# Attention and MoE kernel on one core: softmax probabilities scaled by other engines, two heads' scores in one pass, new order of work

## Chip, cores and metric

The kernel runs on one core of a Trainium2 chip. The metric is device time in microseconds (us) of one execution; lower is better. TensorE (PE) multiplies matrices, PEld is its loading of stationary operands, VectorE is DVE, ScalarE is ACT, GpSimd is POOL, and SP only issues DMAs.

## The reference, cut to what matters

Four batches, eight heads, 576 rows of 64 elements. Each head has causal softmax attention plus a memory read; the sum passes through a two-matrix block.

```python
scores = scale * np.matmul(q, k.transpose(0, 1, 3, 2))      # causal mask, softmax -> a
local = np.matmul(a, v)
q_p = phi(q)                                                # elu(q) + 1
mem_out = einsum(q_p, M_prev) / (einsum(q_p, z_prev) + 1e-6)
x = g * mem_out + (1 - g) * local                           # [2304, 512] after the heads are joined
h = x @ w_in                                                # 512 -> 2048
y = (np.maximum(h, 0) + alpha * np.minimum(h, 0)) @ w_out   # 2048 -> 512
```

## The kernel before

**Numbers.** Most matrix products are made of three or two f16 products of a high and a low half (`hi`, `lo`), because f16 streams through PE faster than f32. Early work, for which the weights and scales are not yet there, is done in plain f32: the first 64 rows of all batches (group Z), batch 0's scores, its first row blocks' transposes and values, and the first half (j < 4) of the MoE of the groups Z and (0, 1).

**Units.** A unit is (batch b, head h, two row blocks: [1, 2] or [3, 4]); there are 64. `unit_scores` (L825) makes both blocks' scores in PSUM, has DVE add the mask and find the minimum (`tensor_tensor_reduce` into the tile `E`), and ACT take the exponential with the row sum in `sm`. Batch 0's scores are f32 products over 64 rows of the array, one head after the other, in the PSUM tiles `s1` (512 words) and `s2` (1024 words). `unit_probs` (L866) finds 1/sum on DVE, and then POOL does two things for each block: it writes q's features times `nrm` into 64 columns of `E`, and it scales the exponentials by the reciprocal. ACT then casts all of `E` to f16 (`P[:, 0]`), DVE subtracts it for the low half (`P[:, 1]`), and SP issues a transposing DMA into `PT`. The units (0, h, [1, 2]) have no halves: PE transposes `E` into `s2`, ACT copies it out. `E` has two buffers of 1152 words. `pair_values` (L901) multiplies `PT` with the values for two heads in the PSUM tile `bank`, and the result goes through another transposing DMA to the group's `x`.

**MoE.** A group is 256 rows: (b, 1) and (b, 3) for each batch, and Z. `moe_in` (L1019) and `moe_out` (L1059) make one of eight steps j of a group. The weights arrive as raw pieces s = 0 to 15 (first half of the hidden width 0 to 7, second half 8 to 15). `conv_w(s)` (L575) makes f32 of piece s in `R[s+1]`, and `split_w(s)` (L607) makes its two f16 halves from `R[s+1]` in `fin(s)` = `R[s]`. So split s writes over the raw piece s-1, and the sixteen splits follow each other from 0 to 15. Steps j >= 4 of Z and (0, 1) need the second half's splits; all later groups need both halves.

**Order.** Operations are not issued as written. `Work.add` (L134) records each with its dependencies (a whole PSUM tile at once), `price` (L182) gives it a duration, `lay` (L241) lays all operations on the five queues, and `issue` (L308) orders them by rank plus the offsets of `STAGES` (L32), two passes forward and one back between them. The result is one fixed order for each engine's queue.

Of the kernel before, what the change touches and what calls it, by code (L numbers as in the profile page):

```python
# [33 lines left out]
        "A0": 11.3, "A:DVE": -217.6, "BK0": -98, "BK:ACT": 124.3, "BK:PE": -853.4, "C0": -90.5, "C1": 150,  # L34
        "C2": -98.2, "C3": -196.5, "C:DVE": 47.3, "C:PE": 107.6, "I": -14.7, "I:POOL": -120.8, "J": -112.4,
        "J:ACT": 4.9, "J:DVE": 0.6, "J:PE": -33.7, "K": -70.4, "K:POOL": 54.3, "L0K:DMA": 52.5, "L0Q": 2,
# [19 lines left out]
        "s33": 401.7, "s:ACT": 20.5, "s:DVE": 100, "s:PE": -311.2, "sZ": -745.5, "sZ:DVE": 63.5, "sZ:PE": 340.6,  # L56
# [4 lines left out]
        "y:DMA": -1030.3, "y:DVE": -62.5, "y:PE": 4032.8,  # L61
# [40 lines left out]
class Work:  # L102
# [30 lines left out]

    def add(self, kind, engine, name, a, kw):  # L134
# [10 lines left out]
        for x, write in [(x, False) for x in ins] + [(x, True) for x in outs]:  # L145
            if x.tensor.name in self.fixed:
                continue
            m, size = self.cells(x)
            if x.space == PSUM:

                m = (1 << 2 * size) - 1
            wrote, read = self.state.setdefault(x.tensor.name, ([], []))
            deps.update(o for o, c in wrote if c & m)
            if not write and x.space == PSUM:
                deps.update(o for o, c in read if self.ops[o][0] != kind)
            if not write:
                read.append((me, m))
                continue
            deps.update(o for o, c in read if c & m)
            for was in (wrote, read):  # L160
                was[:] = [(o, c & ~m) for o, c in was if c & ~m]
            wrote.append((me, m))
        deps.discard(me)
        if last:
# [4 lines left out]
            self.ops.append((kind, both, (a[0],), {}, deps, last[5] + 6, *last[6:]))  # L169
# [12 lines left out]
    def price(self, kind, name, outs, ins, kw):  # L182
# [34 lines left out]
        if kind == "POOL":  # L217
            if name == "tensor_scalar":
                return 150 + 1.55 * n
# [21 lines left out]
    def lay(self, before, after, rank, back=False):  # L241
# [11 lines left out]
        turn, used, warm = WINDOW, 0.0, False  # L253
# [4 lines left out]
        while todo:  # L258
# [49 lines left out]
    def issue(self, tc):  # L308
# [15 lines left out]
        for passes, bias in STAGES:  # L324
            rank = [x + 1e3 * (bias.get(op[7], 0) + bias.get(op[7].rstrip("0123456789_") + ":" + op[0], 0))
                    for x, op in zip(rank, ops)]
# [13 lines left out]
def kernel(  # L340
# [49 lines left out]
    o_sc = bank[:, 256:512]  # L390
    ident = cp.tile([128, 128], F32, name="ident")
# [31 lines left out]
    def fin(pos):  # L423
        return R[pos].bitcast(F16)
# [132 lines left out]
    wkp.made["E"] = [0, [E[:, 1152 * i:1152 * i + 1152] for i in range(2)]]  # L557
    E = E[:, 0:2048]
# [264 lines left out]
    flip = [0]  # L823

    def unit_scores(b, h, bl):  # L825
        work.phase = f"s{b}{bl[0]}"
        p = pre[b]
        a = h % 2
        width = [64 + 128 * i for i in bl]
        mx = smp.tile([128, 2], F32, tag="mx", bufs=3, name=f"mx{b}_{h}_{bl[0]}")  # L830
        sm = smp.tile([128, 2], F32, tag="sm", bufs=3, name=f"sm{b}_{h}_{bl[0]}")
        f32 = b == 0 and bl[0] == 1
        E = wkp.tile([128, 1152], F32, tag="E", name=f"E{b}_{h}_{bl[0]}")
        flip[0] ^= 1
        if sum(width) > 512:
            s1 = psp.tile([128, 512], F32, tag="s1", name=f"sa{b}_{h}")
            s2 = psp.tile([128, 1024], F32, tag="s2", name=f"sb{b}_{h}")
            where = [s1[:, 0:width[0]], s2[:, 0:width[1]]]
        else:
            u = 0 if f32 else flip[0]  # L840
            ps = psp.tile([128, (512, 1024)[u]], F32, tag=("s1", "s2")[u])
            where = [ps[:, 0:width[0]], ps[:, width[0]:sum(width)]]
        if b:
            qT, qS, k1, _ = stacks[b, h // 2]
            terms = [(qT[:, a], k1[:, a]), (qS[:, a], k1[:, a])]
        else:
            terms = [(x[64 * a:64 * a + 64, h // 2] for x in (p["qT"], p["kT"]))]
        terms = [tuple(x) for x in terms]
        for i, w, s in zip(bl, width, where):
            for c0 in range(0, w, 512):  # L850
                c1 = min(c0 + 512, w)
                for j, (x, y) in enumerate(terms):
                    T.matmul(s[:, c0:c1], lhsT=x[:, (i - 1) * 128:i * 128],
                             rhs=y[:, 64 + c0:64 + c1], start=(j == 0), stop=(j == len(terms) - 1))
        es, o = [], 0
        for j, (w, s) in enumerate(zip(width, where)):
            o += 64
            es.append(E[:, o:o + w])
            V.tensor_tensor_reduce(out=es[j], in0=s, in1=mask[:, 576 - w:576], op0=ALU.add, op1=ALU.min,
                                   scale=p["nse"] if b else -0.125, scalar=3.0e38, accum_out=mx[:, j:j + 1])  # L860
            o += w
        for j, e in enumerate(es):
            A.activation(e, e, AF.Exp, bias=mx[:, j:j + 1], scale=-1.0, accum_out=sm[:, j:j + 1])
        ust[b, h, bl[0]] = (sm, es, E)

    def unit_probs(b, h, bl):  # L866
        work.phase = f"P{b}{bl[0]}"
        p = pre[b]
        sm, es, E = ust.pop((b, h, bl[0]))
        nb = len(bl)  # L870
        V.scalar_tensor_tensor(out=sm, in0=sm, scalar=1e-9, in1=p["C"][:, h, bl[0] - 1:bl[-1]],
                               op0=ALU.add, op1=ALU.mult)
        V.reciprocal(sm, sm)
        ns = sum(i + 1 for i in bl)
        s0 = 0
        for j, i in enumerate(bl):
            G.tensor_scalar(E[:, s0 * 128:s0 * 128 + 64], nat[b]["q"][i - 1][:, h], p["nrm"][:, i - 1, h:h + 1], None,
                            op0=ALU.mult)
            G.tensor_scalar(es[j], es[j], sm[:, j:j + 1], None, op0=ALU.mult)
            s0 += i + 1  # L880
        if b == 0 and bl[0] == 1:
            PT = wkp.tile([128, 9, 128], F32, tag="PT", bufs=TB)
            pt = psp.tile([128, 1024], F32, tag="s2")[:, 0:128 * ns]
            for c in range(ns):
                T.transpose(pt[:, c * 128:c * 128 + 128], E[:, c * 128:c * 128 + 128], ident)
            A.copy(PT[:, 0:ns].rearrange("p s c -> p (s c)"), pt)
# [4 lines left out]
        E = E[:, 0:ns * 128]  # L891
        A.copy(P[:, 0], E)
# [444 lines left out]
```

## Time and profile before

| what | value |
|---|---|
| median of 3 runs | 629.15 us (624.66 to 632.19) |
| the profiled execution | 629.02 us, of which the span of the instructions is 627.2 us |
| mean granted TensorE clock | 0.965 of full |
| PE busy in the span | 566.9 us |
| DVE, ACT, POOL busy | 449.7, 357.8, 260.0 us |

Busy time of PE is the union of its records, whose ends are modelled; matmuls overlap in the pipeline, so the distance from start to start tells what one really takes. "Idle before" is time in which the engine had nothing running, with the operation that ended it.

### The profile page before, as it was taken

What the parts mean: (1) busy time and instruction counts of PE and PEld (TensorE: products, weight loads), DVE (VectorE), ACT (ScalarE), POOL (GpSimd) and SP (SyncE); (2) the same over time, 40 slices, a digit from 0 to 9 for tenths busy, and PEclk for the clock granted to TensorE, in tenths of its full rate; (3) what the DMA queues carried; (4) which work ended last, traced back from release to release, by engine and by line L of the source; (5) the groups of instructions that cost most, each with busy time, mean ns of one, the idle gap of its engine ahead of it and who ended that gap; (6) DMA issues with size and microseconds to landing.
All of it is one profiled execution on the core that took longest, in us unless ns stands there. A gap on an engine that the chain in (4) does not pass through costs nothing. (4 is left out here: it accounts for less than half of the span.)

```text
span 627.2 us, 11994 instructions
## 1 busy us (share of the span) xinstructions
PE 566.9 (90%) x4421; PEld 365.8 (58%) x4421; DVE 449.7 (72%) x1141; ACT 357.8 (57%) x710; POOL 260.0 (41%) x270
## 2 busy tenths in 40 slices
PE   9858999799899889988998798979889899999997
PEld 4447644463377556556665576557457566666663
DVE  2797898869878989888887888776766775323242
ACT  4437747647678736757466765576655664332222
POOL 2000486564543025655656652565676665000000
PEclk9958999999879999999999999998999999999999
DMA  7899555764359784656996942578725653210000
GB/s 215 217 306 222 174 168 150 205 148 106 84 125 197 172 210 100 127 96 143 178 221 146 191 86 55 118 152 168 152 56 102 130 119 86 47 43 0 18 18 33
DMA packets 226026, 82.84 MB, mean 132 GB/s; under 512 B 216224, under 2 KB 216240, under 8 KB 225968
## 3 DMA queue, kind: packets, MB, share of 16 engines
q1 hardware_dynamic: 225968, 82.09, 57.6%
q8 instruction: 34, 0.56, 0.4%
q14 instruction: 24, 0.20, 0.1%
HBM read 35.66 MB, written 5.77 MB: 66 GB/s over the span
## 5 line engine op out<-in xcount | busy, mean ns | idle before, releaser
L336 PE MATMUL h<-x,R 128*128 128x256 f16 x1536 | 264.2, 276 | 18.6 <-DVE r L336 13.6
L336 PE MATMUL y<-R,gg 128*128 128x512 f16 (+1 forms) x832 | 258.3, 400 | 5.0 <-ACT gg L336 3.8
L336 POOL TENSOR_SCALAR E<-E,sm 128x192 f32<-128x192 f32 (+3 forms) x128 | 184.0, 1450 | 90.6 <-DVE sm L336 62.5
L336 PE MATMUL bank<-v,PT 128*128 128x64 f16 x1224 | 186.9, 195 | 10.2 <-DVE xn L336 9.1
L336 PEld LDWEIGHTS <-R 128*128 128x128 f16 x1536 | 149.4, 99 | 58.5 <-DVE r L336 20.7
L336 POOL TENSOR_SCALAR E<-q,nrm 128x64 f32<-128x64 f32 x128 | 72.1, 576 | 181.6 <-DVE nrm L336 66.7
L336 PEld LDWEIGHTS <-PT 128*128 128x128 f16 x1224 | 116.5, 99 | 17.4 <-issue 10.9
L336 PEld LDWEIGHTS <-gg 128*128 128x128 f16 x768 | 74.6, 98 | 85.5 <-issue 7.5
L336 DVE TENSOR_TENSOR P<-E,P 128x1152 f16<-128x1152 f32 (+1 forms) x56 | 63.1, 1127 | 55.4 <-ACT P L336 55.4
L336 ACT CAST P<-E 128x1152 f16<-128x1152 f32 (+1 forms) x56 | 54.2, 968 | 84.4 <-POOL E L336 81.0
L336 ACT ACTIVATE E<-E,mx 128x192 f32<-128x192 f32 (+3 forms) x128 | 77.7, 608 | 35.8 <-DVE mx L336 35.6
L336 DVE SCALAR_TENSOR_TENSOR gg<-r,gsc,gg 128x512 f16<-128x512 f32 x56 | 42.1, 752 | 40.7 <-ACT gg L336 40.2
L336 PE MATMUL s<-k,qT 128*128 128x192 f16 (+8 forms) x200 | 66.6, 376 | 4.3 <-DVE mx L336 4.3
L336 DVE SCALAR_TENSOR_TENSOR r<-r,oma,h 128x256 f32<-128x256 f32 x128 | 55.9, 475 | 19.7 <-ACT r L336 19.3
L336 ACT ACTIVATE gg<-r,gsc 128x512 f16<-128x512 f32 x56 | 40.1, 717 | 47.7 <-PE y L336 46.2
L336 DVE CUSTOM_DVE_ANT_0 E<-s,mask,pm 128x320 f32<-128x320 f32 (+2 forms) x96 | 56.6, 611 | 5.0 <-PE s L336 4.3
L336 ACT ACTIVATE r<-h 128x512 f32<-128x512 f32 x72 | 42.0, 589 | 27.3 <-DVE gg L336 13.1
L336 PE MATMUL h<-R 128*128 128x256 f32 x128 | 34.8, 414 | 4.5 <-ACT R L336 3.4
L336 PE MATMUL s<-k,qS 128*128 128x192 f16 (+4 forms) x120 | 33.9, 294 | 0.3 <-DMA qS<-qT 0.3
L336 PEld LDWEIGHTS h<-R 128*128 128x128 f32 x128 | 25.1, 210 | 10.1 <-ACT R L336 4.5
L336 ACT ACTIVATION_READ_ACCUMULATOR E<-E,mx 128x1 f32 x128 | 24.1, 188 | 0.0
L336 PE MATMUL h<-ones 128*128 128x512 f16 x66 | 21.3, 423 | 1.0 <-DVE ones L336 1.0
(173 smaller groups left out, 614.5 us busy)
## 6 DMA issues: line engine op xcount, KB each, us to landing
vn<-in_v_dram SPq DMA_DIRECT2D x16, 256.0 KB, 4.2
q<-in_q_dram SPq DMA_DIRECT2D x16, 256.0 KB, 5.4
out_dram<-t SPq DMA_DIRECT2D x16, 256.0 KB, 2.2
kn<-in_moe_w_in_dram SPq DMA_DIRECT2D x6, 512.0 KB, 5.8
kn<-in_moe_w_out_dram SPq DMA_DIRECT2D x6, 512.0 KB, 4.3
kn<-in_k_dram SPq DMA_DIRECT2D x12, 256.0 KB, 4.3
qS<-qT SPq DMA_DIRECT2D x24, 128.0 KB, 2.9
R<-in_moe_w_in_dram SPq DMA_DIRECT2D x4, 512.0 KB, 6.9
```

What stands on the lines that cost most here:

```text
L336: fn(*a, **kw)
```

## The change

1. `unit_probs`: POOL no longer scales the exponentials. It writes only the features, now with two scalar factors (`nrm` and the sum times the constant `sm`), and the reciprocal goes to a second tile `rs`. ACT scales while it writes the high half and DVE scales while it subtracts, each in two instructions, one a block, instead of one for both. For the units (0, h, [1, 2]) ACT scales the f32 exponentials in place.
2. `first_pair`: batch 0's scores of two heads are issued side by side, head a on array rows 64a to 64a+63, in different PSUM banks. For [3, 4] block 4 of one head stands beside block 3 of the other.
3. PSUM: `s1` and `s2` become one tile `SS` of three banks, and dependencies in PSUM are kept by bank. Blocks [1, 2] of later batches and the two steps of group Z take turns in the three banks. The f32 transposes go through one bank in two portions (four and one).
4. `E` of the units (0, h, [1, 2]) gets five tiles of 640 words: three in the old place and the two `P` buffers.
5. `fin(0)` moves to `R[16]` and `fin(8)` to `R[0]`; batch 0's f32 `x32` moves from `R[16]` to `R[0]`. `weights(1)` with its splits 8 to 15 now stands ahead of `splits(0)` and `splits(4)`, and the chain of overwrites runs from 8 to 15 and then 0 to 7.
6. The planner prices POOL's `tensor_scalar` at 290 + 2.55 n instead of 150 + 1.55 n ns, adds a price for changing between whole-array and partial-array matmuls, and has a second set of offsets, by phase and engine. All queues get another order.

```diff
 STAGES = [
     (2, {
-        "A0": 11.3, "A:DVE": -217.6, "BK0": -98, "BK:ACT": 124.3, "BK:PE": -853.4, "C0": -90.5, "C1": 150,
+        "A0": -271.6, "A:DVE": -630.1, "BK0": 128.2, "BK:ACT": 57.8, "C0": -243.2, "C1": 111.2, "C2": -388.2,
...
+    (1, {
+        "A0": -7.3, "A0:DVE": -0.1, "A:DVE": 26.5, "BK0": -47.7, "BK0:ACT": 3.9, "BK0:PE": -0.6, "BK:ACT": 7.7,
...
-            m, size = self.cells(x)
-            if x.space == PSUM:
-
-                m = (1 << 2 * size) - 1
+            m = self.banks(x) if x.space == PSUM else self.cells(x)[0]
...
-                return 150 + 1.55 * n
+                return 290 + 2.55 * n
...
+                    if packets != mode:
+                        hold += (95 if packets else 0) + (0, 0, 150, 200)[mode]
+                    mode = packets
...
     def fin(pos):
-        return R[pos].bitcast(F16)
+        return R[{0: 16, 8: 0}.get(pos, pos)].bitcast(F16)
...
+    wkp.made["E3"] = [0, [E[:, 768 * i:768 * i + 640] for i in range(3)] + [x[:, 0:640] for x in wkp.made["P"][1]]]
...
+    def first_pair(hp, bl):
+        work.phase = f"s0{bl[0]}"
+        p = pre[0]
+        tiles = [unit_tiles(0, 2 * hp + a, bl) for a in range(2)]
+        for j in range(2):
+            cols = []
+            for a in range(2):
+                i = bl[j if bl[0] == 1 else a ^ j ^ 1]
+                w = 64 + 128 * i
+                o = 512 * a + 192 * j if bl[0] == 1 else 1024 if i == 3 else 0
+                cols.append((a, i, SS[:, o:o + w]))
+            cols.sort(key=lambda x: -x[2].shape[1])
+            for c0 in (0, 512):
+                for n, (a, i, row) in enumerate(cols):
+                    c1 = min(c0 + 512, row.shape[1])
+                    if c1 <= c0:
+                        continue
+                    x, y = (p[t][64 * a:64 * a + 64, hp] for t in ("qT", "kT"))
+                    work.paired = n == 1
+                    T.matmul(row[:, c0:c1], lhsT=x[:, (i - 1) * 128:i * 128], rhs=y[:, 64 + c0:64 + c1],
+                             start=True, stop=True)
+            for a, i, row in cols:
+                es, mx, _ = tiles[a]
+                e = i - bl[0]
+                lowest(0, row, es[e], mx[:, e:e + 1])
...
-            G.tensor_scalar(E[:, s0 * 128:s0 * 128 + 64], nat[b]["q"][i - 1][:, h], p["nrm"][:, i - 1, h:h + 1], None,
-                            op0=ALU.mult)
-            G.tensor_scalar(es[j], es[j], sm[:, j:j + 1], None, op0=ALU.mult)
+            G.tensor_scalar(E[:, s0 * 128:s0 * 128 + 64], nat[b]["q"][i - 1][:, h], p["nrm"][:, i - 1, h:h + 1],
+                            None if f32 else sm[:, j:j + 1], op0=ALU.mult, op1=ALU.bypass if f32 else ALU.mult)
+            if f32:
+                A.activation(es[j], es[j], AF.Copy, scale=rs[:, j:j + 1])
+            segs.append(slice(s0 * 128, (s0 + i + 1) * 128))
...
-        A.copy(P[:, 0], E)
-        V.tensor_tensor(P[:, 1], E, P[:, 0], op=ALU.subtract)
+        for j, c in enumerate(segs):
+            A.activation(P[:, 0, c], E[:, c], AF.Copy, scale=rs[:, j:j + 1])
+            V.scalar_tensor_tensor(out=P[:, 1, c], in0=E[:, c], scalar=rs[:, j:j + 1], in1=P[:, 0, c],
+                                   op0=ALU.mult, op1=ALU.subtract)
...
-            groups[b, i].update(x32=R[13 if b else 16].rearrange("p (a c) -> p a c", a=NP), halves=True)
+            groups[b, i].update(x32=R[13 if b else 0].rearrange("p (a c) -> p a c", a=NP), halves=True)
...
     halve(gz)
     halve(g0)
+    weights(1)
     splits(0)
     splits(4)
-    weights(1)
     do(sum(load_batch(1), []))
```

## Rows read from the trace of the kernel before

**Rows 1.** The page: busy time, share of the span, instructions, by engine.

```profile
PE 566.9 (90%) x4421; PEld 365.8 (58%) x4421; DVE 449.7 (72%) x1141; ACT 357.8 (57%) x710; POOL 260.0 (41%) x270
```

**Rows 2.** Busy by stretch: stretch, length, PE, PEld, DVE, ACT, POOL, clock, DMA, GB/s.

```profile
60.00:200.00 140.00, 131.77 (x710) 75.74 (x709) 120.11 (x291) 95.03 (x177) 72.00 (x64) 0.94 0.61 152
200.00:340.00 140.00, 125.39 (x1122) 83.71 (x1121) 120.34 (x326) 87.79 (x177) 68.30 (x75) 1.00 0.74 158
340.00:540.00 200.00, 178.69 (x1748) 123.21 (x1746) 142.10 (x364) 120.29 (x248) 115.44 (x120) 0.98 0.58 117
540.00:627.20 87.20, 83.43 (x569) 52.32 (x566) 26.63 (x52) 25.50 (x39) 0.00 (x0) 1.00 0.06 20
```

**Rows 3.** The same view: opening, 161 to 181 us, 100 to 120 us.

```profile
0.00:60.00 60.00, 47.62 (x282) 30.81 (x283) 40.50 (x112) 29.19 (x73) 4.23 (x13) 0.83 0.89 240
...
161.00:181.00 20.00, 17.59 (x106) 9.31 (x105) 13.45 (x32) 11.31 (x17) 13.37 (x12) 0.66 0.46 109
...
100.00:120.00 20.00, 17.22 (x76) 8.05 (x73) 19.20 (x52) 12.44 (x30) 15.01 (x13) 1.00 0.77 226
```

**Rows 4.** PE's waits, 200 to 540 us: total, times, longest.

```profile
PE h L336 <- DVE r L336: 13.6, 14, 1.9
PE bank L336 <- DVE xn L336: 9.7, 10, 2.5
```

**Rows 5.** PE in order of time, at 167 us: start, length, operation, idle before.

```profile
167.46 0.61 PE L336 MATMUL h<-x,R 128*128 128x256 f16 x2 [1.67 <-ACT R L336]
```

**Rows 6.** Groups by shape, PE: batch 0's f32 scores; busy us, mean ns, idle.

```profile
L336 PE MATMUL s<-k,qT 64*128 64x448 f32 x16 | 9.0, 643 | 1.1 <-DVE mx L336 1.1
...
L336 PE MATMUL s<-k,qT 64*128 64x320 f32 x16 | 6.4, 481 | 0.0
...
L336 PE MATMUL s<-k,qT 64*128 64x192 f32 x16 | 4.7, 375 | 0.0
```

**Rows 7.** PE in order of time: one score product, then two products on column halves.

```profile
158.68 1.02 PE L336 MATMUL s<-k,qT 64*128 64x448 f32 x2
159.63 0.20 PE L336 MATMUL bank<-v,PT 128*128 128x64 f16 x1
...
86.60 0.43 PE L167 MATMUL bank<-PT,vn 128*64 128x256 f32 x1
86.61 0.43 PE L168 MATMUL bank<-PT,vn 128*64 128x256 f32 x1
```

**Rows 8.** POOL: scaling (page's groups); features (by tile, ns min/median/max).

```profile
L336 POOL TENSOR_SCALAR E<-E,sm 128x192 f32<-128x192 f32 (+3 forms) x128 | 184.0, 1450 | 90.6 <-DVE sm L336 62.5
...
L336 POOL TENSOR_SCALAR E<-q,nrm x128: 436/445/2965, 71.7 to 521.6; 128x64 f32<-128x64 f32 x128
```

**Rows 9.** DVE: page's group of the low half, then groups by shape.

```profile
L336 DVE TENSOR_TENSOR P<-E,P 128x1152 f16<-128x1152 f32 (+1 forms) x56 | 63.1, 1127 | 55.4 <-ACT P L336 55.4
...
L336 DVE SCALAR_TENSOR_TENSOR q<-q,scr,q 128x512 f16<-128x512 f32 x12 | 8.8, 744 | 0.2 <-ACT q L336 0.2
...
L336 DVE SCALAR_TENSOR_TENSOR k<-kn,scr,k 128x640 f16<-128x640 f32 x12 | 10.5, 884 | 0.1
...
L336 DVE SCALAR_TENSOR_TENSOR R<-R,wsc 128x1024 f16<-128x1024 f32 x16 | 20.9, 1307 | 1.3 <-ACT R L336 0.9 <-PE bank L336 0.4
...
L336 DVE CUSTOM_DVE_ANT_0 E<-s,mask 128x576 f32<-128x576 f32 x8 | 6.0, 750 | 0.0
```

**Rows 10.** ACT: page's group of the high half, then groups by shape.

```profile
L336 ACT CAST P<-E 128x1152 f16<-128x1152 f32 (+1 forms) x56 | 54.2, 968 | 84.4 <-POOL E L336 81.0
...
L336 ACT ACTIVATE q<-q,scr 128x512 f16<-128x512 f32 x12 | 8.4, 712 | 0.0
...
L336 ACT ACTIVATE k<-kn,scr 128x640 f16<-128x640 f32 x12 | 9.7, 819 | 1.4 <-DVE scr L336 1.4
```

**Rows 11.** By tile: the low half on DVE, ns min/median/max, first and last start.

```profile
L336 DVE TENSOR_TENSOR P<-E,P x56: 812/1350/1359, 130.3 to 534.2; 128x1152 f16<-128x1152 f32 x32, 128x640 f16<-128x640 f32 x24
```

More of the change, by code (lines that the diff above doesn't have):

```diff
@@ new lines @@
+        "C3": -1232.9, "C:ACT": 6.9, "C:DVE": -1010.6, "C:PE": -155.1, "I:DVE": 74.2, "I:POOL": 455.7,
[9 rows of a table added]
+        "P:DMA": -611.7, "P:DVE": -1203.9, "P:PE": -63, "P:POOL": 139.7, "S0": 5563.1, "S1": -1561.9, "S3": -1827.9,
+        "S:ACT": 91.8, "S:DVE": 248, "V0": -1.2, "V:PE": -55.7, "a0": -645.8, "a1": -2.3, "a2": -2, "a3": 458.7,
+        "a4": 395.9, "a:ACT": -1239, "a:DVE": -1609.6, "bk0": -153.9, "bk1": 135.1, "bk2": -2.6, "bk3": -1.5,
+        "bk:ACT": -1438.9, "bk:DMA": -473.7, "bk:DVE": -477.6, "bk:PE": -584.5, "bv0": 174, "bv1": 65.7, "bv2": 2.6,
[5 rows of a table added]
@@ new lines @@
+        "o31": -1071.1, "o33": -466.4, "o:ACT": -431.9, "o:DMA": 29.3, "o:DVE": -726.2, "o:PE": -469.3, "oZ": -11.6,
+        "oZ:ACT": -1559.9, "oZ:DVE": -1291.2, "oZ:PE": -81.7, "p1": -2914.9, "p2": -286.9, "p3": -715.7, "p4": 13.8,
+        "p:ACT": -1229.2, "p:DVE": -633.5, "q1": 61.7, "q2": -1110, "q3": 59, "q:ACT": -234.1, "q:DVE": -671.8,
[7 rows of a table added]
+        "y:DVE": -1121.7, "y:PE": 639.6,
+    }),
[4 rows of a table added]
+        "C:ACT": -20.6, "C:DVE": -11.7, "C:PE": 37.9, "I": 6.7, "I:POOL": 1.3, "J": 1.8, "J:ACT": -11.3,
[12 rows of a table added]
+        "P33:DVE": 1.3, "P33:POOL": 14.4, "P:ACT": -9.2, "P:DMA": -16.7, "P:DVE": -12.2, "P:PE": 14.4, "P:POOL": 4.9,
[6 rows of a table added]
+        "bk:ACT": -23.9, "bk:DMA": 2, "bk:DVE": -13.2, "bk:PE": 28.8, "bv0:ACT": -10.3, "bv0:DVE": -13, "bv1": -0.4,
[12 rows of a table added]
+        "h4_11:DVE": -11.2, "h4_11:PE": 46.8, "h:ACT": -8.7, "h:DVE": -12.2, "h:PE": 45.7, "n": 4, "n:PE": 0.2,
[5 rows of a table added]
+        "o33:PE": 1.8, "o:ACT": -22.9, "o:DMA": -16.1, "o:DVE": -13.2, "o:PE": 46, "oZ": 3.1, "oZ:ACT": 0.2,
[9 rows of a table added]
+        "s33:PE": 48.3, "s:ACT": 6, "s:DVE": -12.2, "s:PE": 45.5, "sZ": 7.1, "sZ:DVE": -0.4, "sZ:PE": 0.3,
[13 rows of a table added]
+        "y:DVE": -11.7, "y:PE": 45.5,
@@ L132, in cells, with banks @@
         return sum(m << size * h for h in range(2) if p0 < 64 * (h + 1) and p0 + pn > 64 * h), size
+    def banks(self, ap):
+        (ps, pn), *free = ap.ap
+        o = ap.offset % ps
+        return (2 << (o + sum(st * (n - 1) for st, n in free)) // 512) - (1 << o // 512)
     def add(self, kind, engine, name, a, kw):
@@ L168, in both @@
                 second[0](*second[1], **second[2])
-            self.ops.append((kind, both, (a[0],), {}, deps, last[5] + 6, *last[6:]))
+            hold = max(last[5], self.price(kind, name, outs, ins, kw)) + (60 if ins[0].shape[0] == 64 else 6)
+            self.ops.append((kind, both, (a[0],), {}, deps, hold, *last[6:8], (0.0, 1.0, False, last[8][3])))
             return
@@ L175, in add @@
             late = ins[0].shape[0] / 128
+            x = kw.get("lhsT")
+            packets = 0 if x is None else 1 if x.shape[0] == 64 else 3 if x.shape[0] < 64 else 2 if outs[0].shape[0] == 64 else 0
         elif kind == "DVE":
@@ L324, in issue @@
         for passes, bias in STAGES:
-            rank = [x + 1e3 * (bias.get(op[7], 0) + bias.get(op[7].rstrip("0123456789_") + ":" + op[0], 0))
-                    for x, op in zip(rank, ops)]
+            rank = [x + 1e3 * sum(bias.get(k, 0) for k in dict.fromkeys((
+                op[7], op[7].rstrip("0123456789_") + ":" + op[0], op[7] + ":" + op[0]))) for x, op in zip(rank, ops)]
             for n in range(passes):
@@ L390, with third @@
     o_sc = bank[:, 256:512]
+    SS = psp.tile([128, 1536], F32, tag="s")
+    turns = [0]
+    def third():
+        turns[0] += 1
+        return SS[:, turns[0] % 3 * 512:turns[0] % 3 * 512 + 512]
     ident = cp.tile([128, 128], F32, name="ident")
@@ L822, with unit_tiles @@
     ust = {}
-    flip = [0]
+    def unit_tiles(b, h, bl):
+        w = 640 if (b, bl[0]) == (0, 1) else 1152
+        E = wkp.tile([128, w], F32, tag="E3" if w == 640 else "E", name=f"E{b}_{h}_{bl[0]}")
+        mx = smp.tile([128, 2], F32, tag="mx", bufs=3, name=f"mx{b}_{h}_{bl[0]}")
+        sm = smp.tile([128, 2], F32, tag="sm", bufs=3, name=f"sm{b}_{h}_{bl[0]}")
+        es, o = [], 0
+        for i in bl:
+            o += 64
+            es.append(E[:, o:o + 64 + 128 * i])
+            o += 64 + 128 * i
+        ust[b, h, bl[0]] = (sm, es, E, mx)
+        return es, mx, sm
@@ new lines, in lowest @@
+    def lowest(b, s, e, mx):
+        w = s.shape[1]
+        V.tensor_tensor_reduce(out=e, in0=s, in1=mask[:, 576 - w:576], op0=ALU.add, op1=ALU.min,
+                               scale=pre[b]["nse"] if b else -0.125, scalar=3.0e38, accum_out=mx)
+    def first_pair(hp, bl):
[23 more added lines that the diff above has]
+                lowest(0, row, es[e], mx[:, e:e + 1])
+        for es, mx, sm in tiles:
+            for j, e in enumerate(es):
+                A.activation(e, e, AF.Exp, bias=mx[:, j:j + 1], scale=-1.0, accum_out=sm[:, j:j + 1])
@@ L825, in unit_scores @@
     def unit_scores(b, h, bl):
+        if b == 0:
+            if h % 2:
+                first_pair(h // 2, bl)
+            return
         work.phase = f"s{b}{bl[0]}"
-        p = pre[b]
         a = h % 2
         width = [64 + 128 * i for i in bl]
[L830 to L838, printed above, removed]
-        else:
[L840 to L847, printed above, removed]
@@ L848, in unit_scores @@
-        terms = [tuple(x) for x in terms]
+        es, mx, sm = unit_tiles(b, h, bl)
+        if bl[0] == 1:
+            ps = third()
+            where = [ps[:, 0:width[0]], ps[:, width[0]:sum(width)]]
+        else:
+            where = [SS[:, 0:width[0]], SS[:, 512:512 + width[1]]]
+        qT, qS, k1, _ = stacks[b, h // 2]
         for i, w, s in zip(bl, width, where):
@@ L851, in unit_scores @@
                 c1 = min(c0 + 512, w)
[L852 to L861, printed above, removed]
+                for j, x in enumerate((qT, qS)):
+                    T.matmul(s[:, c0:c1], lhsT=x[:, a, (i - 1) * 128:i * 128], rhs=k1[:, a, 64 + c0:64 + c1],
+                             start=(j == 0), stop=(j == 1))
+        for j, s in enumerate(where):
+            lowest(b, s, es[j], mx[:, j:j + 1])
         for j, e in enumerate(es):
             A.activation(e, e, AF.Exp, bias=mx[:, j:j + 1], scale=-1.0, accum_out=sm[:, j:j + 1])
-        ust[b, h, bl[0]] = (sm, es, E)
     def unit_probs(b, h, bl):
@@ L882, in unit_probs @@
             PT = wkp.tile([128, 9, 128], F32, tag="PT", bufs=TB)
[L883 to L886, printed above, removed]
+            for c0 in range(0, ns, 4):
+                c1 = min(c0 + 4, ns)
+                pt = SS[:, 1024:1024 + 128 * (c1 - c0)]
+                for c in range(c0, c1):
+                    T.transpose(pt[:, (c - c0) * 128:(c - c0) * 128 + 128], E[:, c * 128:c * 128 + 128], ident)
+                A.copy(PT[:, c0:c1].rearrange("p s c -> p (s c)"), pt)
             ust[b, h, bl[0], "T"] = PT[:, 0:ns]
```

27 lines of the change are left out of this document (7 added, 20 removed), and 99 rows, old and new, of the table STAGES.

## The prediction

> **What bounds the kernel now.** I read the page's busy times first: PE runs 90% of the span, DVE 72%, ACT 57%, POOL 41% [rows 1]. Then the same by stretch [rows 2]: after 540 us PE works 83.4 of 87.2 us with DVE at 31%, so the tail is pure matrix work and PE's. From 60 to 540 us PE is busy 131.8 + 125.4 + 178.7 = 435.9 of 480 us and DVE 120.1 + 120.3 + 142.1 = 382.6. In the first 280 of these DVE has 240.4 us, 86%: two engines are nearly full there. The end is thus PE's work plus PE's idle and slow time, and DVE limits how far the first half can shrink. PE's waits from 200 to 540 us [rows 4] show who ends them: DVE's `r` (13.6 us) and DVE's `xn` (9.7), 23.3 of the 340 - 304.1 = 35.9 us that PE idles there. Why is DVE late while it has idle time? Its low-half subtraction stood idle 55.4 us for ACT [rows 9], and ACT's cast stood idle 81.0 us for POOL [rows 10], which needs 1.45 us for each of 128 scalings [rows 8]. One late engine at the head of in-order queues is handed on to PE. Last, the stretch 161 to 181 us [rows 3]: PE's granted clock is 0.66 of full and its MoE matmuls wait for the split weights `R` [rows 5].
>
> **The change, part by part.**
>
> *Scores in pairs (-12 us, bounds 0 and -14.6).* Two heads share the time of one. For [1, 2] half of the 320- and 192-column groups goes: (6.4 + 4.7) / 2 = 5.55 us; for [3, 4] the 448 columns go under the other head's 512: 9.0 us [rows 6]. That is 14.55 us of busy time. Records overlap their successors: a 448 product takes 0.95 us from start to start, against 9.0 / 8 = 1.125 us by busy time [rows 7], so 14.55 x 0.845 = 12.3. No row shows two *row* halves at once; two *column* halves do start 10 ns apart and take 0.43 us together [rows 7]. I take 12, as that is the nearest row; the lower bound is nothing.
>
> *PSUM by bank (+1 us, bounds 0 and +16).* The second half of a pair writes banks that DVE must first have read. DVE reads 576 columns in 0.750 us [rows 9], 1.30 ns each; each head has 192 + 320 + 448 + 576 = 1536 columns, all eight 12,288, so 16.0 us in all. Exposed, behind a waiting score stand all later matmuls of PE's queue. The cover is the f32 MoE of Z and (0, 1), and the scores before already waited in this way for only 1.1 us in the 448 group [rows 6]. The transposes in two portions add one short copy a unit on ACT. I take 1.
>
> *POOL's scaling moves.* POOL loses 184.0 us [rows 8] and keeps 128 features of 0.445 us, 57 us; the second factor of the feature is not shown and sits on an engine with room. DVE: a subtraction with a scalar, f32 to f16, takes 744 ns at 512 and 884 at 640 columns [rows 9], 1.094 a column, so 464 at 256 and 604 at 384. The 32 units [3, 4] cost 1.628 us, the 24 units [1, 2] 1.068: 52.1 + 25.6 = 77.7, against 63.1 now [rows 9]: +14.6 us. ACT: 712 and 819 ns [rows 10], 0.836 a column, hence 498 and 605: 32 x 1.531 + 24 x 1.103 = 75.5 against 54.2, +21.3; and the eight f32 units add 0.445 + 0.552 us each, +8. ACT was busy 303.1 of 480 us [rows 2]; with 29 more it is at 69% and off the path. What is gained is latency: two scalings of 1.45 us and their queueing no longer stand between DVE's reciprocal and ACT's write. DVE's `P` and what is queued behind it (`r`, `xn`, the next minimum) come earlier. The waits on `r` and `xn` are 23.3 us; bounds 0 and -23; I take half, -12, because part of them is plain DVE load that grows.
>
> *Does POOL's leaving free DVE?* The longest low-half subtraction took 1359 ns with a median of 1350 [rows 11], while POOL's feature went from 436 to 2965 ns [rows 8]: POOL is stretched, DVE's records are not. I count nothing. The Trainium skill, page "SBUF — State Buffer", section "Who interferes with whom", says that a DVE instruction with two SBUF inputs contends with a GpSimd instruction that reads SBUF, and that whichever comes first blocks the other for its whole length. By that rule DVE would be given time too: were each of the 56 subtractions waiting half a scaling, an estimate is 56 x 0.73 = 41 us, DVE's price below would vanish and the sum would be 599 instead of 603.
>
> *Second half's weights first (-7 us, bounds 0 and -9).* Z's and (0, 1)'s steps j >= 4 need splits 8 to 15, which now stand behind 0 to 7 in the chain of overwrites and so behind the end of the f32 MoE that reads the raw pieces. In the 20 us of this seam PE idles 2.4 us, and a clock of 0.66 means 13.6 us at half rate, 6.8 us lost [rows 3]: 9.2 together. The stall goes to splits 0 to 7, which the group (0, 3) needs next: 8 x 1.307 = 10.5 us of DVE [rows 9], hidden by the eight steps j >= 4 of Z and (0, 1); without that cover up to 10.5 us would come back. I take 7. The pieces' loads move with them on SP's queue; in the opening the DMA engines are 0.89 busy [rows 3], the bytes stay, and I count 0 there (5 either way).
>
> *DVE's price (+4 us, bounds 0 and +14.6).* From 60 to 340 us PE would like to shrink by 12 - 1 + 7 and its share of the waits (14.6 of 35.9 us idle, so 5 of 12): 23 us. DVE has 240.4 us there and half of the 14.6 added, 247.7. The fullest stretch I found holds 19.2 of 20 us [rows 3]; at 95% DVE needs 260.7 of 280 us. Only 19 can go; 4 come back. After 340 us DVE is at 71% and hides the rest.
>
> *`E3` and the new order.* A pair fills two tiles at once, and five let the next pair start while the last is still being scaled; without them the pairing's 12 us would wait on ACT. So they are costed with the pairing, at nothing of their own. The new order has no row of before; I count 0, and its scatter is in the range.
>
> **Sum.** -12 + 1 - 12 - 7 + 4 = -26. The profiled execution took 629.0 us (span 627.2 and 1.8 around it), and the median is 629.15, so the two agree: 629 - 26 = 603 us, with 594 to 612 as this case's own range.
>
> **Rivals.**
> 1. *All of it.* Pairing 12, the seam 9, all of the 23 us of waits, and DVE's price 5: 590 us. For it: one cause, POOL, stands behind those waits. Against: DVE would need 97% of the first half.
> 2. *Row halves run one after the other*, so the pairing does not do what it says: the 12 fall away, DVE's price too: 629 + 1 - 7 - 12 = 611 us. For it: no row shows two row halves together. Against: the column halves do overlap [rows 7].
> 3. *The time returns in new waits*: pairs with exposed bank reads (up to 16) and splits 0 to 7 without cover (10.5) use up the 26: 629 us. For it: both are on DVE, the fuller engine. Against: PE has other f32 work throughout that stretch (131.8 of 140 us).
> 4. *DVE is the bound and time is lost.* Place: 60 to 540 us. Its work grows from 382.6 to 397.2 us. If its share stays at 382.6 / 480 = 79.7%, the stretch takes 498 us, +18: 647. It decides from a share of 82.8% down (no gain); below 81.7% the kernel is slower by over 1%; I put it at 640. For it: 86% in both halves of the first 280 us looks like a limit. Against: the named cause of DVE's idling is taken out. The Trainium skill, page "TensorEngine Tiling (Array Packing)", section "PSUM Bottleneck", speaks for this rival: tiling makes the matmuls faster, not the reading out of PSUM, which may then bound.
>
> **Chances.** The forecast 0.52, rival 1 0.15, rival 2 0.17, rival 3 0.09, rival 4 0.07. Faster by over 1% (below 623, about what a measurement of this kernel can tell) is the first three, 0.84; within 1% rival 3, 0.09; slower rival 4, 0.07. The range 585 to 624 leaves out rivals 3 and 4 save an edge, and the lowest edge of rival 1: about 0.19.
>
> **What would show it.** Pairing: score products over 64 rows start two at a time, the 448-column one within some 10 ns of a 512-column one; if the second starts 0.9 us after the first, rival 2. Scaling: POOL near 60 us, DVE near 464, ACT near 387; ACT's and DVE's `P` no longer wait 81 and 55 us; PE's waits on `r` and `xn` near 12. Seam: no stretch of half clock between the f32 and the f16 MoE. DVE's share from 60 us to the tail above 85%; at 80% rival 4 holds. I would be wrong above all if DVE, not POOL, makes `r` and `xn` late, or if the new order opens a hole that no row of before shows.

## Result and profile after

The changed kernel takes 585.39 us (median of 4, 584.66 to 586.18) against 628.16 us (median of 4, 624.66 to 632.19): a ratio of 0.9317, 95% interval 0.9257 to 0.9378, or 43 us less. Forecast were 603 us and 26 us less.

First the page of the kernel after: busy time by engine, which answers [rows 1].

```profile
PE 541.5 (93%) x4421; PEld 356.6 (61%) x4421; DVE 456.0 (78%) x1197; ACT 380.7 (65%) x790; POOL 81.6 (14%) x142
```

PE is busy 25.4 us less and idle 19 us less (582.8 - 541.5 = 41.3 against 627.2 - 566.9 = 60.3). DVE has grown by 6.3 us only. Next the kernel after by stretch, with the columns of [rows 2]; the stretch 161 to 181 answers [rows 3].

```profile
0.00:60.00 60.00, 42.91 (x286) 28.75 (x288) 47.43 (x126) 31.00 (x77) 4.22 (x13) 0.80 0.92 257
60.00:200.00 140.00, 131.10 (x835) 78.87 (x836) 126.35 (x327) 106.81 (x216) 24.91 (x33) 0.98 0.66 161
161.00:181.00 20.00, 18.95 (x194) 13.10 (x195) 18.29 (x46) 18.02 (x34) 2.87 (x5) 1.00 0.92 182
200.00:340.00 140.00, 135.06 (x1226) 92.23 (x1224) 132.66 (x377) 109.00 (x234) 27.85 (x50) 1.00 0.76 167
340.00:500.00 160.00, 153.26 (x1534) 106.03 (x1534) 124.63 (x321) 110.60 (x230) 24.64 (x46) 1.00 0.59 122
500.00:582.80 82.80, 79.14 (x548) 50.72 (x546) 24.98 (x49) 23.30 (x36) 0.00 (x0) 0.99 0.06 22
```

The tail of pure matrix work, which the windows put at 500 us here and at 540 us before, is about as long and begins 40 us earlier. In the middle more is done in the same time: between 200 and 340 us PE ran 1226 matmuls where it ran 1122, and DVE is busy 95% where it was 86%. PE idled 11.7 of the 300 us from 200 to 500, where it had idled 35.9 of 340. PE's waits in that stretch, which answer [rows 4], are down to one line:

```profile
PE s L417 <- DVE mx L417: 11.1, 20, 0.8
```

The waits on `r` and `xn` are gone; the one left is on DVE's reading of the scores, and it has grown: in the same stretch of the kernel before it was 2.7 us. Now the page's groups of the work that was moved, answering [rows 8 to 10].

```profile
L417 POOL TENSOR_SCALAR E<-q,nrm,sm 128x64 f32<-128x64 f32 x112 | 69.0, 630 | 277.8 <-DVE sm L417 173.4
L417 DVE SCALAR_TENSOR_TENSOR P<-E,mx,P 128x384 f16<-128x384 f32 (+3 forms) x112 | 75.4, 699 | 5.9 <-ACT P L417 5.3
L417 ACT ACTIVATE P<-E,mx 128x384 f16<-128x384 f32 (+3 forms) x112 | 70.6, 673 | 10.0 <-POOL E L417 7.9
```

ACT waits 7.9 us for POOL instead of 81.0, and DVE 5.3 us for ACT instead of 55.4. Last the pair: the kernel after on PE in order of time.

```profile
116.39 1.04 PE L242 MATMUL s<-k,qT 64*128 64x512 f32 x1
116.40 1.36 PE L243 MATMUL s<-k,qT 64*128 64x448 f32 x2
```

An f32 product is recorded as two instructions. The product of the other head, on the other row half, starts 10 ns after the first.

### The profile page after: what moved, and what is told of

Same layout as the page of the kernel before. It is cut to its first block, busy times and chain, and to the rows that moved or that the text cites. A ratio compares the mean times of both kernels' runs of the same rounds, so it can differ in the third digit from the quotient of the medians.

```text
span 582.8 us, 12013 instructions
## 1 busy us (share of the span) xinstructions
PE 541.5 (93%) x4421; PEld 356.6 (61%) x4421; DVE 456.0 (78%) x1197; ACT 380.7 (65%) x790; POOL 81.6 (14%) x142
## 4 chain that ended last, share of the span: by engine, by line
PE 62%; DVE 16%; ACT 8%; issue 5%; DMA 5%; POOL 2%; SPq 2%; POOLq 0%; DVEq 0%; ACTq 0%
PE y L417 24%; PE h L417 24%; PE s L417 7%; PE bank L417 4%; DVE E L417 4%; DVE P L417 3%; POOL E L417 2%; DMA E<-in_moe_w_in_dram 2%; SPq L417 2%; DVE r L417 2%; DVE gg L417 1%; DVE R L417 1%; ACT r L417 1%; PE s L242 1%; ACT q L417 1%
## 5 line engine op out<-in xcount | busy, mean ns | idle before, releaser
L417 PE MATMUL h<-x,R 128*128 128x256 f16 x1536 | 256.2, 273 | 1.5 <-DVE r L417 1.4
L417 PE MATMUL y<-R,gg 128*128 128x512 f16 (+1 forms) x832 | 254.3, 397 | 1.3 <-ACT t L417 0.7
L417 POOL TENSOR_SCALAR E<-q,nrm,sm 128x64 f32<-128x64 f32 x112 | 69.0, 630 | 277.8 <-DVE sm L417 173.4
L417 ACT ACTIVATE E<-E,mx 128x320 f32<-128x320 f32 (+3 forms) x136 | 81.0, 601 | 30.1 <-DVE mx L417 26.1
L417 DVE SCALAR_TENSOR_TENSOR P<-E,mx,P 128x384 f16<-128x384 f32 (+3 forms) x112 | 75.4, 699 | 5.9 <-ACT P L417 5.3
L417 ACT ACTIVATE P<-E,mx 128x384 f16<-128x384 f32 (+3 forms) x112 | 70.6, 673 | 10.0 <-POOL E L417 7.9
L417 DVE CUSTOM_DVE_ANT_0 E<-s,mask,pm 128x320 f32<-128x320 f32 (+3 forms) x96 | 57.4, 611 | 11.0 <-PE s L417 9.2
L417 PE MATMUL s<-k,qT 128*128 128x64 f16 (+5 forms) x136 | 36.4, 294 | 5.9 <-DVE mx L417 5.6
L417 ACT ACTIVATION_READ_ACCUMULATOR E<-E,mx 128x1 f32 x124 | 23.3, 188 | 0.0
L417 ACT ACTIVATE R<-R,wsc 128x1024 f16<-128x1024 f32 x16 | 18.3, 1143 | 7.5 <-PE h L417 3.6
L417 ACT ACTIVATE t<-y,u 128x512 f32<-128x512 f32 x18 | 12.2, 680 | 13.2 <-PE y L417 13.0
```

The lines of the kernel that those rows point to most:

```text
L417: fn(*a, **kw)
```

## Experiments

Three theories were set against each other. A: POOL's scaling was late in the chain reciprocal, POOL, ACT, DVE, and everything queued behind it on ACT and DVE came late to PE. B: the new order, not the moved work, closed the waits. C: POOL's load itself slowed DVE, wherever it stands.

| run | what it is | median us | ratio to before, 95% interval |
|---|---|---|---|
| after | the change | 585.4 | 0.932, 0.926 to 0.938 |
| e1 | after, both heads on one row half | 590.1 | 0.942, 0.936 to 0.949 |
| e2 | after, extra POOL work in the chain | 636.6 | 1.015, 1.008 to 1.023 |
| e3 | after, extra POOL work aside | 617.3 | 0.982, 0.976 to 0.987 |
| e4 | after, POOL scales, replanned | 629.4 | 1.000, 0.997 to 1.004 |
| e5 | as e3, both pieces together | 637.2 | 1.014, 1.008 to 1.020 |
| e6 | as e5, work that only writes | 621.7 | 0.990, 0.987 to 0.993 |
| e7 | before, scaling moved alone | 592.9 | 0.943, 0.937 to 0.948 |
| e8 | after, old offsets | 588.1 | 0.937, 0.933 to 0.942 |
| e9 | as e5, behind both features | 599.9 | 0.952, 0.948 to 0.958 |
| e10 | after, first half split first | 631.1 | 1.003, 1.000 to 1.006 |
| e11 | e4 with the old offsets | 622.3 | 0.986, 0.980 to 0.993 |
| e12 | after, two E tiles | 594.2 | 0.943, 0.934 to 0.952 |

Each run was timed beside the kernel before, whose median there was between 627.9 and 630.6 us; the ratios go by these, so differences of medians between runs are good to about 3 us.

### What the scaling alone is worth (e7, e11, e4, e8)

e7 puts the new `unit_probs` arithmetic into the kernel before and nothing else (the planner lays the order anew):

```diff
-            G.tensor_scalar(es[j], es[j], sm[:, j:j + 1], None, op0=ALU.mult)
...
-        A.copy(P[:, 0], E)
-        V.tensor_tensor(P[:, 1], E, P[:, 0], op=ALU.subtract)
+        for j, c in enumerate(segs):
+            A.activation(P[:, 0, c], E[:, c], AF.Copy, scale=rs[:, j:j + 1])
+            V.scalar_tensor_tensor(out=P[:, 1, c], in0=E[:, c], scalar=rs[:, j:j + 1], in1=P[:, 0, c],
+                                   op0=ALU.mult, op1=ALU.subtract)
```

> The kernel before with one part of the change alone: ACT and DVE scale, POOL makes only the features; old prices, old offsets, scores one head after the other. Theory A (POOL's scaling was the cause of the late DVE): most of the gain is here without the new order, 595 to 610 us, PE's waits on r and xn under 12 us. Rival B (the gain needs the new offsets): 618 us or more.

592.9 us: 35 of the 43 us, with the old prices, the old offsets and the scores one head after the other. It is a little faster than A expected and rules B out. The last three of PE's waits from 200 to 540 us in e7, and its stretches 60 to 200 and 161 to 181:

```profile
PE bank L336 <- DVE st L336: 1.2, 1, 1.2
PE bank L336 <- DVE xn L336: 1.1, 1, 1.1
PE h L336 <- DVE r L336: 0.6, 2, 0.4
```

```profile
60.00:200.00 140.00, 135.19 (x814) 80.34 (x813) 129.02 (x329) 112.50 (x218) 24.98 (x33) 1.00 0.59 149
161.00:181.00 20.00, 17.49 (x215) 12.80 (x215) 19.78 (x46) 17.97 (x34) 4.76 (x5) 1.00 0.61 137
```

`r` and `xn` fell from 23.3 us to 1.7. And the stretch of low clock at 161 to 181 us is gone, with a clock of 1.00 from 60 to 200 us throughout, although the weights are split in the old order.

e11 is the other corner: all of the change except the scaling and the offsets. e4 is the same with the new offsets.

```diff
-            if f32:
-                A.activation(es[j], es[j], AF.Copy, scale=rs[:, j:j + 1])
+            G.tensor_scalar(es[j], es[j], rs[:, j:j + 1], None, op0=ALU.mult)
...
-        for j, c in enumerate(segs):
...
+        A.copy(P[:, 0], E)
+        V.tensor_tensor(P[:, 1], E, P[:, 0], op=ALU.subtract)
```

> All of the change but the scaling and the offsets: POOL scales as before, the offsets are those of before, and the pairs, the banks, the five E tiles, the weights' order and the new prices stay. Theory A (the scaling is some 35 of the 43 us, the rest adds to it): 612 to 622 us. Rival (the other parts only pay once POOL is out of the chain): 625 us or more.

> The changed kernel with the old way of scaling (POOL scales by the reciprocal, one cast on ACT and one subtraction on DVE for a unit), priced and ordered by the new planner with the new offsets. Theory A: the waits come back even when planned for, 598 to 612 us, with DVE's busy time 15 us lower. Rival B (the old planner's price of POOL was the fault, not POOL's work): under 592 us.

622.3 and 629.4 us. So prices nearer to what POOL takes do not bring the gain: with POOL in the chain ACT still waits for it, here in e4:

```profile
ACT P L417 <- POOL E L417: 44.8, 31, 4.2
```

e11 is at the top of what A expected; e4 lies 17 us above the top for it and 7 us over e11: the new offsets do harm when POOL is back. DVE's busy time in e4 did not fall by the 15 us that A expected: it is 456.5 us against 456.0 in the change, although its low half takes 64.4 us there and 75.4 in the change. e8 keeps the change and takes only the offsets back:

```diff
 STAGES = [
     (2, {
-        "A0": -271.6, "A:DVE": -630.1, "BK0": 128.2, "BK:ACT": 57.8, "C0": -243.2, "C1": 111.2, "C2": -388.2,
+        "A0": 11.3, "A:DVE": -217.6, "BK0": -98, "BK:ACT": 124.3, "BK:PE": -853.4, "C0": -90.5, "C1": 150,
```

> The changed kernel with the offsets of the kernel before (one set), all else as changed. Theory A: 590 to 605 us, the offsets are worth 5 to 20 us. Rival B (the gain is the order's): 610 us or more.

588.1 us, a little below A's range. With the old offsets the four corners are:

| | POOL scales | ACT and DVE scale |
|---|---|---|
| the rest as before | 628.2 | 592.9 (e7) |
| the rest as after | 622.3 (e11) | 588.1 (e8) |

The scaling is worth 35 and 34 us by the medians (36 and 31 by the ratios), all other parts together 6 and 5 (9 and 3), and the new offsets 2.7 more (585.4). The intervals of e7 and e8 overlap, as do those of e8 and the change, so how the rest divides between the other parts and the offsets is not clear.

### Where POOL's work hurts: place or load (e2, e3, e5, e6, e9)

These keep the order of the change on PE, DVE, ACT and SP and add, after split 7, some 90 POOL instructions of about the old sizes (in e6 180 shorter ones). In e2 they multiply the exponentials by one, in the chain:

```diff
+                    feature(*a, **kw)
+                    if split_done:
+                        nc.gpsimd.tensor_scalar(e, e, ones[:, 0:1], None, op0=ALU.mult)
```

> The changed kernel in the same order, but after split 7 POOL also multiplies each block's exponentials by 1.0 behind its feature, some 91 extra POOL instructions of 0.8 to 1.8 us between the reciprocal and ACT's high half. Theory A (POOL's latency in the chain made DVE late): ACT's wait on POOL grows from 8 to 50 us or more, PE's waits on DVE return by 10 us or more, total 595 to 612 us. Rival B (the new order closed the waits, the chain's latency is hidden): under 590. Rival C (POOL's load itself slows DVE through a shared port): as much here as with the extra work aside.

ACT's wait on POOL is 67.2 us and PE's waits on `r` and `xn` are back at 12.3, as A expected; the largest of PE's waits is now the one on `mx`, 31.8 us against 11.5 in the change. The total is 636.6 us, 51 more than the change and 25 above A's range, and more than in e11 (622.3), where POOL does all 128 scalings: an order that was planned without this work takes it worse than one that knows of it. In e3 nothing waits for the result:

```diff
+                        nc.gpsimd.tensor_scalar(R[8][:, 0:e.shape[1]], mask[:, 0:e.shape[1]], ones[:, 0:1], None, op0=ALU.mult)
```

> The same order and the same number, size and place of extra POOL instructions, but they read the mask and write a spare tile, so that nothing waits for their result (a later feature still stands behind them on POOL's queue). Theory A: only POOL's own queueing remains, 585 to 591 us. Rival C (shared port): DVE's two-input instructions get longer by over 3% and the total lies within 3 us of the run with the work in the chain.

617.3 us fits neither A (591 at most) nor C (within 3 us of e2). The reason is in the queue: the unit's second feature stands behind the first block's extra work, and ACT waits for that feature.

```profile
ACT P L417 <- POOL E L1010: 45.3, 41, 2.5
```

e5 was to move both pieces behind block j = 1's feature:

```diff
+                        if j:
+                            for x in es:
+                                nc.gpsimd.tensor_scalar(R[8][:, 0:x.shape[1]], mask[:, 0:x.shape[1]], ones[:, 0:1], None,
+                                                        op0=ALU.mult)
```

> As the run with POOL's extra work aside (617.3 us), with the same 90-odd instructions reading the mask and writing a spare tile, but both of a unit come behind the unit's second feature, so that no feature of the same unit stands behind them. Theory A (what costs is POOL's lateness in the chain, here its queue): ACT's wait on POOL falls from 45 to under 20 us and the total to 585 to 595 us. Rival C (POOL's load slows DVE through a shared port): the total stays at 605 us or more although ACT no longer waits.

637.2 us. The edit missed its aim: on POOL's queue the larger block j = 1 usually comes first, so that both pieces now stood in front of the other feature. e5 on POOL in order of time:

```profile
299.82 0.96 POOL L1010 TENSOR_SCALAR E<-q,nrm,sm 128x64 f32<-128x64 f32 x1 [3.92 <-DVE sm L417]
300.77 3.39 POOL L1014 TENSOR_SCALAR R<-mask,ones 128x448 f32<-128x448 f32 x2
304.15 0.76 POOL L1010 TENSOR_SCALAR E<-q,nrm,sm 128x64 f32<-128x64 f32 x2
```

A feature is 3.4 us late, and ACT's wait on POOL is 66.4 us. A and C were to part by whether ACT still waits, so their forecasts are not put to the test here; but beside e9 the run is the cleanest measure of place, and beside e6 of what reading does. e6 has the same place and work that reads nothing:

```diff
+                                for half in range(2):
+                                    nc.gpsimd.memset(R[8][:, 0:2 * x.shape[1] - 192], 0.0)
```

> As the run before it, but POOL's extra work is setting the spare tile to zero (it reads nothing), twice a block, of about the same length in all. Theory A: 585 to 595 us, as with the extra work that reads. Rival C (a port for reads): faster than the run with reads by over 5 us.

621.7 us, far above A's range for the same reason as e5. It is 15.5 us faster than e5, as C expected, but its POOL is also 22 us less busy in all (184.0 against 206.0), so the 15.5 us are not reading alone. e9 then counts the features of a unit and adds the work of e5 when both are out:

```diff
+                        tally[b, h, bl[0]] = tally.get((b, h, bl[0]), 0) + 1
+                        if tally[b, h, bl[0]] == 2:
+                            for x in es:
+                                nc.gpsimd.tensor_scalar(R[8][:, 0:x.shape[1]], mask[:, 0:x.shape[1]], ones[:, 0:1], None,
+                                                        op0=ALU.mult)
```

> In the run with the extra work aside and late (637.2 us) the second block's feature turned out to come first on POOL's queue, so the extra work still stood in front of the other feature. Here it stands behind both features of its unit; same order, same reads of the mask and writes of a spare tile. Theory A (lateness in the chain is what costs): ACT's wait on POOL falls under 25 us and the total to 586 to 602 us, the rest being units that follow each other closely. Rival C (POOL's reading slows DVE through a shared port): DVE's records are 6 to 8 us longer as in the other two runs, and the total stays at 610 us or more.

599.9 us. POOL is as busy as in e5 (205.0 and 206.0 us), and the kernel is 37 us faster. ACT's waits, e5 and then e9:

```profile
ACT P L417 <- POOL E L1010: 66.4, 44, 3.3
```

```profile
ACT P L417 <- POOL E L1010: 25.0, 21, 2.5
```

So most of what POOL's work costs is its place. 14.5 us are left over the change; they are shared by ACT's wait that is still 17 us longer than in the change and by DVE's longer instructions, which the next lines show: DVE's low half of 640 columns in the change, in e9 and e5 (POOL reads) and in e6 (POOL only writes, at the place of e5).

```profile
L417 DVE SCALAR_TENSOR_TENSOR P<-E,mx,P 128x640 f16<-128x640 f32 x32 | 28.2, 882 | 1.2 <-ACT P L417 1.1
```

```profile
L417 DVE SCALAR_TENSOR_TENSOR P<-E,mx,P 128x640 f16<-128x640 f32 x32 | 30.9, 965 | 0.9 <-ACT P L417 0.9
```

```profile
L417 DVE SCALAR_TENSOR_TENSOR P<-E,mx,P 128x640 f16<-128x640 f32 x32 | 29.4, 918 | 0.2 <-ACT P L417 0.2
```

```profile
L417 DVE SCALAR_TENSOR_TENSOR P<-E,mx,P 128x640 f16<-128x640 f32 x32 | 28.1, 879 | 1.6 <-ACT P L417 1.5
```

DVE's busy time in all is 456.0 us in the change and 459.0 in e6; in the four runs whose extra work reads it is 8 to 11 us more than in the change (465.2 in e2, 463.8 in e3, 464.7 in e5, 466.9 in e9). C is thus real and small; how the 14.5 us divide between the two was not settled.

### The pair, its tiles, and the weights' order (e1, e12, e10)

e1 keeps the order and puts both heads on rows 0 to 63:

```diff
-                    x, y = (p[t][64 * a:64 * a + 64, hp] for t in ("qT", "kT"))
+                    x, y = (p[t][0:64, hp] for t in ("qT", "kT"))
```

> The changed kernel in the same order on every queue, but both heads of a pair use array rows 0 to 63 (odd heads get even heads' scores, so their output is wrong), so that two score products cannot run at once. Theory: the pairing gains because two row halves run together; the 16 products of 448 columns and half of those of 192 and 320 come back into PE's time, 11 to 14 us, to 596 to 600 us. Rival (the gain is in the order, the row halves run one after the other anyway): within 2 us of the changed kernel's 585.4.

PE in order of time in e1, where the pair of the change started 10 ns apart:

```profile
117.60 1.12 PE L242 MATMUL s<-k,qT 64*128 64x512 f32 x2
118.57 0.91 PE L243 MATMUL s<-k,qT 64*128 64x448 f32 x2
```

The second product starts 0.97 us later, so the row halves do run together in the change. The whole pair takes 1.81 us from start to start here (117.60 to 119.41) and 1.05 in the change (122.53 to 123.58), both at full clock (the pair shown above is partly at the lower one). PE's busy time grows by 7.9 us (541.5 to 549.4), the kernel by 4.7 us (6.5 by the ratios): more than the rival's 2 us and half or less of what was expected.

e12 gives the units (0, h, [1, 2]) two tiles:

```diff
-    wkp.made["E3"] = [0, [E[:, 768 * i:768 * i + 640] for i in range(3)] + [x[:, 0:640] for x in wkp.made["P"][1]]]
+    wkp.made["E3"] = [0, [E[:, 1152 * i:1152 * i + 640] for i in range(2)]]
```

> The changed kernel with two tiles instead of five for the units of batch 0, blocks [1, 2], replanned. If the tiles carry the pairing: 589 us or more, PE waiting for ACT or DVE before 120 us. Rival (the f32 MoE covers it): within 3 us of 585.4.

The two runs took 591.2 and 597.1 us, 6 and 12 us more than the change; the intervals touch, so the size is rough, but it is no less than what e1 lost without the overlap. In e12 PE is busy 127.58 us of the stretch 60 to 200 against 131.10. From 100 to 120 us it is busy 14.78 us at a clock of 0.77, in the change 16.48 at 0.83. PE's wait on ACT's copies `PT` is 3.4 us against 2.4, so the expected wait is hardly named there.

e10 takes back the weights' order:

```diff
-        return R[{0: 16, 8: 0}.get(pos, pos)].bitcast(F16)
+        return R[pos].bitcast(F16)
...
+    splits(0)
+    splits(4)
     weights(1)
-    splits(0)
-    splits(4)
```

> The changed kernel with the weights' splits and the place of batch 0's f32 x as before (0 to 7 ahead of 8 to 15), replanned with the new offsets. Theory A (this part is worth the seam's 7 us): 590 to 597 us, with a stretch of low clock or idle PE between the f32 and f16 MoE. Rival (the seam was closed by the earlier P, not by this part): within 3 us of 585.4.

631.1 us, outside both expectations. By stretch, e10:

```profile
60.00:200.00 140.00, 111.20 (x583) 63.55 (x582) 120.52 (x318) 101.07 (x206) 19.49 (x33) 0.89 0.62 154
160.00:180.00 20.00, 11.81 (x110) 8.50 (x112) 19.60 (x48) 18.62 (x35) 1.50 (x4) 0.70 0.66 148
```

A hole opens where PE is busy 11.8 of 20 us at a clock of 0.70 while DVE is full. But this is no clean measure: the new offsets hold splits 0 to 3 back (`"S0": 5563.1`), which suits a chain in which they come behind splits 8 to 15 and probably stops one in which they come first. What the weights' order is worth by itself stays open; at the old offsets it is one of the parts that give about 5 us together (e7 to e8).

## Why the prediction was right or wrong

**The way and the range were right; the size was not.** 585.4 lies 0.4 us inside the lower edge of 585 to 624, less than the scatter of its four runs (584.7 to 586.2): that it lies inside is luck. It is below the forecast's own 594 to 612. Nearest is rival 1 (590 us, chance 0.15), which took the waits on `r` and `xn` whole, as the runs show; DVE held 259.0 of 280 us from 60 to 340 us, 92% and not the 97% that stood against it. The share that DVE must hold for rival 4 to fail was 82.8%: it held 126.35 + 132.66 + 124.63 = 383.6 of 440 us from 60 to 500 us, 87%.

**The term that was mis-sized is the latency of POOL's scaling: -12 forecast, -35 measured for moving the work as a whole (e7).** The mechanism was the one named: ACT waits for POOL, DVE for ACT, PE for DVE. The price was not. I took only the waits on `r` and `xn` that the profile names between 200 and 540 us, and half of them. Both cuts were wrong. Those waits went nearly to nothing (23.3 to 1.7 us in e7); from 60 us to the tail PE idles 16.8 us in e7 where it idled 44.1, so 21.6 of these 27 us are `r` and `xn` and the rest are other waits. The other part is PE's own speed: its busy time fell from 566.9 to 552.7 us, and its granted clock rose from 0.965 to 0.980. At its two levels (1.2 and 2.4 GHz) that is some 44 us at the lower one before and 24 in e7, so as an estimate 10 us of the 14. (In the opening PE idles 5 us more in e7.) How much of the 35 us is lateness and how much DVE's own relief from POOL is not settled: e9, with POOL's work where little waits for it, still loses 14.5 us.

**The seam (-7) is part of it.** The seam is the stretch 161 to 181 us, where the f16 MoE takes over from the f32 MoE. I read PE's wait for the split weights [rows 5] as a matter of the splits' order. The kernel before, on ACT and then on DVE, just ahead of that wait:

```profile
164.44 1.15 ACT L336 CAST P<-E 128x1152 f16<-128x1152 f32 x1 [4.01 <-POOL E L336]
165.50 0.77 ACT L336 ACTIVATE E<-E,mx 128x576 f32<-128x576 f32 x1
166.18 0.19 ACT L336 ACTIVATION_READ_ACCUMULATOR E<-E,mx 128x1 f32 x1
166.27 1.13 ACT L336 ACTIVATE R<-R,wsc 128x1024 f16<-128x1024 f32 x1
```

```profile
165.63 1.36 DVE L336 TENSOR_TENSOR P<-E,P 128x1152 f16<-128x1152 f32 x1 [1.95 <-ACT P L336]
167.44 1.31 DVE L336 SCALAR_TENSOR_TENSOR R<-R,wsc 128x1024 f16<-128x1024 f32 x1 [0.45 <-ACT R L336]
```

The high half of `R` on ACT, which ended PE's wait, stood behind a cast that had waited 4.01 us for POOL, and the low half of `R` on DVE stood behind a low half that had waited for the same cast. e7, with the old order of the weights, has a clock of 1.00 in these 20 us and in the whole stretch 60 to 200. e11, with the new order of the weights and POOL's scaling, also has 1.00 from 161 to 181 us, but 0.90 from 60 to 200, with PE busy 119.95 us: there slow time came earlier. The gain was there, and I had put it under the wrong edit. That the new order of weights adds nothing to it was not shown.

**Pairs: -12 forecast, -4.7 measured (e1).** That row halves run together was right, and rival 2 falls. The overlap spares 7.9 us of PE's busy time and not 12: a pair of 512 and 448 columns spares 0.76 us where I had 0.95. Of the 7.9 us, 2.7 are idle again in the profiled executions (PE idles 41.3 us in the change, 38.6 in e1). PE's granted clock is also lower in the change than in e1, 0.972 against 0.977, above all at 110 us, behind PE's waits for ACT's `E` (1.58 us in the change, 1.40 in e1). The stretch in the change and then in e1:

```profile
110.00:118.00 8.00, 6.79 (x25) 3.16 (x24) 3.53 (x5) 4.32 (x9) 0.00 (x0) 0.57 0.47 144
```

```profile
110.00:118.00 8.00, 5.65 (x23) 2.76 (x24) 5.23 (x9) 4.87 (x13) 0.00 (x0) 0.79 0.55 173
```

What this slow time costs by itself, and whether a full DVE keeps the rest, no run shows.

**PSUM by bank: +1 forecast.** For the pairs this holds: on batch 0's products PE waited 0.9 us for DVE's reading, 0.5 of it on the paired ones. But I had counted batch 0 alone. The units of later batches, which do not stand in pairs, share the same three banks, and on them PE's wait for DVE's reading is the largest left: 11.1 us from 200 to 500 us, against 2.7 before and 2.1 in e7, both with the old tiles, and 8.7 in e8 and 6.6 in e11, with the new tiles and the old offsets. That the tiles make it is argued from these five runs; none changes the tiles alone. The Trainium skill's section "PSUM Bottleneck" (page "TensorEngine Tiling (Array Packing)") spoke for rival 4, with PSUM's reading as what may bound once products are tiled: the 0.5 us on the paired products do not bear that out here.

**DVE's price.** The two-piece low half costs 75.4 us, 77.7 forecast, so +12.3. DVE as a whole grew by 6.3, so its other work became 6 us shorter. That DVE gets nothing from POOL's leaving was wrong by about this much: in e4, where POOL scales in the changed kernel, DVE's other work is longer than in the change by 11 us of busy time, 8 when its records are added up. What DVE's price of 4 us at the end came to, no run shows. I had looked at the median and the longest of one group [rows 11]; sums over all groups show it. The Trainium skill's rule (page "SBUF — State Buffer", section "Who interferes with whom") names two SBUF inputs on DVE against a GpSimd instruction that reads, not one that only writes; e9 with 965 ns, e5 with 918 and e6 with 879 against 882 agree with it. Its full price as I had estimated it, 41 us, took the block for a whole instruction, which the section spells out for another mode of DVE; the 11 us of e9 are far from it.

**`E3` and the offsets.** The tiles were rightly costed with the pair: without them 6 to 12 us are lost (e12, two runs). The offsets, counted at 0, are worth 2.7 us, no more than can be told.

## What to carry to other kernels

When a slow engine stands in the middle of a chain that crosses in-order queues, its price can be more than the waits that carry its name down to the bound engine. Here these waits, 23.3 us, went nearly whole, 6 us of other waits went with them, and the bound engine's granted clock rose, for 35 us in all. A first estimate should take such waits whole, follow the queues at every other hole of the bound engine, and add the slow time. Giving the work to engines that are already on the chain can pay even if one of them is nearly full, because part of its idle time was waiting. And before taking back a part of a change whose order was tuned with it, take the tuning back too: e4 measures a broken order as well as the part, and e10 probably does.

## What the hardware showed

Two f32 products on the two row halves of the array start 10 ns apart and overlap (512 and 448 columns, against 0.97 us apart on one half). POOL instructions that read SBUF lengthen DVE instructions with two SBUF inputs (640 columns: 882 ns with 82 us of POOL busy, 918 and 965 in e5 and e9 with 206 and 205 us), and those that only write do not (879 ns in e6 with 184 us). POOL's own place in a chain costs far more: the same 90 instructions cost 52 us in front of a feature and 14.5 us behind it.
